# Warm-up products behind the first phase sums, and five in each wait of the output weights' transposes

## The chip, the cores and the metric

The kernel runs on one core of a Trainium2 chip, as one program. The metric is the device time of one execution in microseconds, the median of several runs. The engines are TensorE (PE in the rows; PEld is its weight load), VectorE (DVE), ScalarE (ACT), GpSimd (POOL) and SyncE (SP), which issues the loads and stores.

## The reference

Four batches of 768 tokens with eight heads of 48 go through a recurrence with a complex decay, then through a dense gated layer whose output is linear in two products, and then through a layer with eight experts, of which each token takes one.

```
mag = np.sqrt(a_re * a_re + a_im * a_im)
scale = np.minimum(mag, 0.999) / (mag + 1e-06)
ar, ai = a_re * scale, a_im * scale
S_re, S_im = ar * S_re - ai * S_im + k_t v_t, ar * S_im + ai * S_re     # for each token t
y[t] = q_t @ S_re
x = (x @ w_a) * (x @ w_b) @ w_out                                       # dense layer
do = x @ w_skip > 0                                                     # experts
e = argmax(x @ w_gate); gate = softmax(x @ w_gate)[e]
out = x + do * gate * (relu(x @ w1[e]) @ w2[e])
```

The inputs of the dense layer, w_a, w_b and w_out, arrive as 64-bit floats; the kernel reads them as pairs of 32-bit integers and puts the 32-bit value together itself.

## The kernel before

**The recurrence** is done in chunks of 128 tokens: 24 units of one chunk of one batch (number i), taken as 12 pairs (number g). For a unit, `att_exp` makes the logarithms of the decay and sums them over the tokens on TensorE (bank `l2_i`); `att_trig` makes the phases with Arctan and sums them (bank `tp_i`, line 251), then takes sine and cosine (`ts`) and rotates q and k (`qr`, `kr`, on VectorE). `att_pe` transposes the rotated q and k in two halves (banks `pq` and `pk`, lines 320 and 325), lets ScalarE copy them (`tq`, `tk`, lines 322 and 327), multiplies them to scores (`pc`, line 330), which VectorE masks (`sc`, line 332), and multiplies by v (`y`, line 352; the state's products `ds`, line 303). Three other names: `t1`, `t2`, `t` are its work tiles, `re`, `im` and `imp` its loads.

**The weights of the dense layer** come in 18 chunks, in the order of the words d.. of the string START: six of w_a, six of w_b and six of w_out (a0, b1, b0, o0, a1, o1 and so on). `decode` takes ScalarE (line 381) and three steps of VectorE (lines 382, 386, 387) for one chunk, 128 x 768 elements (tiles `deca`, `decb`, `deco`). `split` then rounds it on ScalarE (line 392, tiles `wa`, `wb`, `wo`) and takes the rest on GpSimd (line 393). Only three tiles serve all decodes in turn, so that the fourth one (deco0) uses the tile of the first (deca0). A decode releases the load of the chunk three places later: `load_after` lets GpSimd copy one element of the decoded tile into the raw tile, and the load waits for that. A chunk of w_out has a tail: TensorE transposes each of its two halves (bank `wt`, three transposes, line 451), ScalarE copies them (`wtt`, line 453), TensorE multiplies the copy by the gate's weights (line 455) and VectorE copies the result (`w2s`, line 456).

**The dense layer** of a pair g is done in 12 steps, m g.0 to m g.11 in START: products of the exchanged tokens `xt` with w_a and w_b (bank `ab`, lines 509 to 511), their product (`asb`, `gh`, `gl`), and the products with w_out (bank `op`). The tokens of a pair are exchanged between partitions by six transfers (`xt<-xt`, line 371).

**What sets the order.** START sets the order in which the code is written; a scheduler then orders each engine's instructions by its own estimates, with the table HOLD, which ties some instructions behind others. Each engine runs its list in that order, and so do the queues of loads on SP and POOL. The groups 0 and 1 and all decodes are in START; the groups from 2 on follow in a loop, in which TensorE has the dense layer of group g and the recurrence of group g + 1 to do.

**Products that nobody reads.** There are two kinds already. With WARM = 2 two products stand behind unit 0's `ts` (line 477, bank `warm`), and `warm(name, ins, n)` puts n bf16 products of 128 x 256 behind an instruction, into a bank "op" (lines 664 to 669); it is used near 730 us, between the dense layer and the experts.

Of the kernel before, what the change touches and what calls it, by code (L numbers as in the profile page):

```python
# [49 lines left out]
FILLP = ()  # L50
WARMS = (10, 6, 24)
WARMX = (13, 8)
ENGINES = {getattr(mybir.EngineType, x) for x in ("PE", "Activation", "DVE", "Pool")}
GF = 5
SGN = ()
# [4 lines left out]
def kern(tc, q, k, v, a_re, a_im, w_a, w_b, w_out, w_skip, w_gate, w1, w2, out):  # L60
# [3 lines left out]
    with st:  # L64
# [8 lines left out]
        def bank(tag, name, bufs):  # L73
            return ps.tile([P, 512], F32, tag=tag, name=name, bufs=bufs)

        env = SimpleNamespace(at=("at", "at2"), n=0)

        def at(name):
            env.n += 1
# [157 lines left out]
        def att_trig(i):  # L237
            c, b = units[i]
            d = U[i]
            im = d["im"]  # L240
            t3 = ew.tile([P, W], F32, tag="t3", name=f"t3_{i}")
            t4 = ew.tile([P, W], F32, tag="t4", name=f"t4_{i}")
            tact(out=t4, in_=im, func=AF.Arctan)
            if c > 0:

                cr = ew.tile([1, W], F32, tag="cr", name=f"cr{i}", bufs=1)
                sync.dma_start(cr, carry[b])
                dve.scalar_tensor_tensor(out=t4[:1], in0=cr, scalar=-2.0 * math.pi, in1=t4[:1], op0=ALU.mult, op1=ALU.add)
            tp = at(f"tp_{i}")
            if i < SPL:  # L250
                pe.matmul(tp[:, :W], trit, t4, start=True, stop=True)
            else:
                hi, lo = parts(i, "t", ("t2", "t1"))
                act.activation(out=hi, in_=t4, func=AF.Copy, scale=INV2PI)
                dve.scalar_tensor_tensor(out=lo, in0=t4, scalar=INV2PI, in1=hi, op0=ALU.mult, op1=ALU.subtract)
                cumsum(tp, hi, lo)

            if i in OFF.get("magic", ()):
                act.activation(out=t3, in_=tp[:, :W], func=AF.Identity, bias=b_magic)
            else:  # L260
                dve.tensor_scalar(out=t3, in0=tp[:, :W], scalar1=MAGIC, scalar2=None, op0=ALU.add)
            dve.scalar_tensor_tensor(out=t3, in0=t3, scalar=MAGIC, in1=tp[:, :W], op0=ALU.subtract, op1=ALU.subtract)
            if c + 1 < NCH:
                carry[b] = dpool.tile([1, W], F32, name=f"carry{i}")
                sync.dma_start(carry[b], t3[127:128])
            if i < 6:
                tact(out=t4, in_=t3, func=AF.Abs)
            else:
                dve.tensor_scalar(out=t4.bitcast(I32), in0=t3.bitcast(I32), scalar1=0x7FFFFFFF, scalar2=None, op0=ALU.bitwise_and)
            tact(out=t4, in_=t4, func=AF.Sin, scale=-TWO_PI_IN, bias=b_hpi)  # L270
            ts = ew.tile([P, W], F32, tag="t1", name=f"ts{i}")
            d["ts"] = ts
            marks["ts", i] = tact(out=ts, in_=t3, func=AF.Sin, scale=-TWO_PI_IN)
            for nm in ("q", "k"):
                tag = "krl" if nm == "k" and i >= 6 and i % 2 else nm + "r"
                r = ew.tile([P, 2 * W + 32], F32, tag=tag, name=f"{nm}r{i}", bufs=1)
                if nm == "k":
                    pool.memset(r[:, 2 * W :], 0.0)
                    d["kf"] = r
                r = r[:, : 2 * W].rearrange("t (h x d) -> t h x d", x=2, d=D)  # L280
                src = d[nm].rearrange("t (h d) -> t h d", d=D)
                off(nm + "c", i).tensor_tensor(out=r[:, :, 0], in0=src, in1=t4.rearrange("t (h d) -> t h d", d=D), op=ALU.mult)
                e = off(nm + "s", i)
                ins = e.tensor_tensor(out=r[:, :, 1], in0=src, in1=ts.rearrange("t (h d) -> t h d", d=D), op=ALU.mult)
                if e is dve:
                    mark((nm + "r", i), ins)
                d[nm + "r"] = r

        xts = {}

        def att_pe(i):
# [2 lines left out]
            qr, kr, vt, ee = d["qr"], d["kr"], d["v"], d["ee"]  # L294
            sc, qT = [], []
            stt = state[b]
            def delta(prev=None):

                ds = at(f"ds{i}")
                for h in range(H):  # L300
                    for x in range(2):
                        l = d["kf"][:, 96 * h + 64 * x : 96 * h + 64 * x + 64]
                        ins = pe.matmul(ds[64 * x : 64 * x + 64, h * D : (h + 1) * D], l, vt[:, h * D : (h + 1) * D], start=True, stop=True).ins
                        if prev is not None:
                            after(ins, prev)
                        prev = ins
                return ds, prev
# [9 lines left out]
            for hh in range(2):  # L317
                pq = at(f"pq{i}_{hh}")
                for j in range(4):
                    pe.transpose(pq[:96, j * P : (j + 1) * P], qr[:, 4 * hh + j].rearrange("t x d -> t (x d)"), ident)  # L320
                tq = ew.tile([96, 512], F32, tag="tq", name=f"tq{i}_{hh}", bufs=2)
                mark(("tq", i, hh), act.activation(out=tq, in_=pq[:96], func=AF.Copy))
                pk = at(f"pk{i}_{hh}")
                for j in range(4):
                    pe.transpose(pk[:96, j * P : (j + 1) * P], kr[:, 4 * hh + j].rearrange("t x d -> t (x d)"), ident)
                tk = ew.tile([96, 512], F32, tag="tk", name=f"tk{i}_{hh}", bufs=2)
                mark(("tk", i, hh), act.activation(out=tk, in_=pk[:96], func=AF.Copy))  # L327
                pc = at(f"pc{i}_{hh}")
                for j in range(4):
                    last = pe.matmul(pc[:, j * P : (j + 1) * P], tk[:, j * P : (j + 1) * P], tq[:, j * P : (j + 1) * P], start=True, stop=True).ins  # L330
                s_ = ew.tile([P, 4, P], F32, tag="sc", name=f"sc{i}_{hh}", bufs=2)
                msk = mark(("sc", i, hh), dve.tensor_tensor(out=s_, in0=pc.rearrange("s (j t) -> s j t", t=P), in1=tri[:, None, :].to_broadcast([P, 4, P]), op=ALU.mult))
                sc.append(s_)
                qT.append(tq)
# [37 lines left out]
            if c + 1 < NCH:  # L372
                new_state(ds)
            del U[i]


        def decode(dst, raw, by_pool, k):
# [57 lines left out]
        def decode_w(k, dec, wtp, ahead=None):  # L435
# [12 lines left out]
            for x in range(2):  # L448
                pt = bank("at2", f"wt{f}_{x}", 2)
                for c in range(NCC):  # L450
                    pe.transpose(pt[:, c * P : (c + 1) * P], d[:, x, c * P : (c + 1) * P], ident)
                wt = wtp.tile([P, DM], F32, tag="cr", name=f"wtt{f}_{x}", bufs=1)
                act.activation(out=wt, in_=pt[:, :DM], func=AF.Copy)
                for c in range(NCC):
                    pe.matmul(pt[:, DM : DM + 10], wt[:, c * P : (c + 1) * P], wg[:, c], start=c == 0, stop=c == NCC - 1)
                dve.tensor_copy(w2[:, x], pt[:, DM : DM + 10])
            split(t[:, 0, :, DM:], t[:, 1, :, DM:], w2)

        def att_exps(p):
            table("natural_log_exp_and_others")  # L460
# [8 lines left out]
        def att_trigs(p):  # L469
            table("trig_and_small")  # L470
            for i in (2 * p, 2 * p + 1):
                att_trig(i)
            if p == 0 and WARM:

                wm = bank("op", "warm", 2)
                for x in range(WARM):
                    pe.matmul(wm[:, :DM], ident, U[0]["ts"], start=True, stop=True)
            for i in (2 * p, 2 * p + 1):
                att_pe(i)


        M = {}
# [18 lines left out]
        def moe1_step(g, f):  # L501
            xt = M[g][0]
            fs = slice((f % 2) * P, (f % 2 + 1) * P)
            ab = bank("ab", f"ab{g}_{f}", 2)
            for x, nm in enumerate("ab"):
                o = ab[:, x * 256 : (x + 1) * 256]
                for c in range(NCC):
                    wh, wl = (env.w[nm, f // 2][:, y, c, fs] for y in range(2))
                    pe.matmul(o, wl, xt[:, c, 0], start=c == 0, stop=False)  # L509
                    pe.matmul(o, wh, xt[:, c, 1], start=False, stop=False)  # L510
                    pe.matmul(o, wh, xt[:, c, 0], start=False, stop=c == NCC - 1)  # L511
            if len(pend) == 2:
                moe1_out(*pend.pop(0))
            asb = env.mp.tile([P, 256], F32, tag="asb", name=f"asb{g}_{f}")
# [146 lines left out]
            if last:  # L661
                warm("t", ins.ins, WARMS[2])

        def warm(name, ins, n):

            if n:
                wm = bank("op", f"warm{name}", 2)
                for x in range(n):
                    after(pe.matmul(wm[:, :CAP], ones, iota, start=True, stop=True).ins, ins)

        giu = cpool.tile([P, 2, NE], U32, name="giu")
        siu = cpool.tile([P, 2, NE], U32, name="siu")
# [241 lines left out]
        moe1_flush()  # L914
        att_next(2)
        env.at = ("at", "at2")
        for g in range(2, NG):
            if g + 1 < NG:
                att_exps(g + 1)
# [186 lines left out]
```

## Time and profile before

| | us |
|---|---|
| median of 3 runs | 889.76 (889.67 to 892.65) |
| profiled execution, its own time | 889.2 |
| profiled execution, span from the first to the last instruction | 887.2 |
| TensorE busy in the span | 830.7 (94%) |
| VectorE busy | 554.3 (62%) |
| ScalarE busy | 466.7 (53%) |
| GpSimd busy | 266.6 (30%) |

The own time holds some 2 us around the span. A busy TensorE is not TensorE at its highest clock: the clock that was granted stands beside it, as a share of 2.4 GHz, so that 0.50 is 1.2 GHz. The first two groups and the decodes fill the stretch up to about 150 us, the rest of the recurrence and of the dense layer that up to about 725, and the experts the rest.

### The profile page before, as it was taken

What the parts mean: (1) busy time and instruction counts of PE and PEld (TensorE: products, weight loads), DVE (VectorE), ACT (ScalarE), POOL (GpSimd) and SP (SyncE); (2) the same over time, 40 slices, a digit from 0 to 9 for tenths busy, and PEclk for the clock granted to TensorE, in tenths of its full rate; (3) what the DMA queues carried; (4) which work ended last, traced back from release to release, by engine and by line L of the source; (5) the groups of instructions that cost most, each with busy time, mean ns of one, the idle gap of its engine ahead of it and who ended that gap; (6) DMA issues with size and microseconds to landing.
All of it is one profiled execution on the core that took longest, in us unless ns stands there. A gap on an engine that the chain in (4) does not pass through costs nothing.

```text
span 887.2 us, 18318 instructions
## 1 busy us (share of the span) xinstructions
PE 830.7 (94%) x7051; PEld 802.6 (90%) x7051; DVE 554.3 (62%) x1293; ACT 466.7 (53%) x977; POOL 266.6 (30%) x313
## 2 busy tenths in 40 slices
PE   2678889999999999999999999999999999999995
PEld 0567778999999999999999999999999889999995
DVE  3789976648567395764947658394753444755551
ACT  5577555646556373564726646374443325455540
POOL 5275543104131020312103130031302214675751
PEclk9687899999999999999999999999999999999998
DMA  9789672223122131221413222120102319767600
GB/s 166 143 159 191 164 108 55 72 45 84 36 72 58 26 92 33 71 59 25 102 26 77 45 72 57 27 73 10 55 1 73 116 40 322 239 218 228 190 16 30
DMA packets 162800, 81.53 MB, mean 92 GB/s; under 512 B 132788, under 2 KB 148730, under 8 KB 162704
## 3 DMA queue, kind: packets, MB, share of 16 engines
q1 hardware_dynamic: 160656, 74.88, 36.0%
q0 software_dynamic: 2048, 5.40, 1.7%
q8 instruction: 57, 0.93, 0.4%
q14 instruction: 39, 0.32, 0.1%
HBM read 66.10 MB, written 12.61 MB: 89 GB/s over the span
## 4 chain that ended last, share of the span: by engine, by line
PE 81%; DMA 7%; DVE 3%; ACT 3%; SPq 2%; issue 2%; POOL 1%; POOLq 0%; DVEq 0%; ACTq 0%
PE ab L509 11%; PE ab L511 10%; PE ab L510 10%; PE op L493 5%; PE op L495 5%; PE op L494 5%; PE y L352 5%; PE pc L330 5%; PE eh L786 3%; PE eh L787 3%; PE eh L789 2%; PE eo L803 2%; PE eo L805 2%; PE eo L804 2%; DMA rawb<-in_moe_w_b_dram 2%; PE pq L320 2%
## 5 line engine op out<-in xcount | busy, mean ns | idle before, releaser
L509 PE MATMUL ab<-xt,wa 128*128 128x256 f32 x432 | 125.6, 291 | 4.4 <-DVE asb L516 2.4
L511 PE MATMUL ab<-xt,wb 128*128 128x256 f32 x432 | 124.2, 288 | 0.0
L510 PE MATMUL ab<-xt,wb 128*128 128x256 f32 x432 | 123.5, 286 | 0.0
L511 PE MATMUL ab<-xt,wa 128*128 128x256 f32 x432 | 123.3, 285 | 0.0
L509 PE MATMUL ab<-xt,wb 128*128 128x256 f32 x432 | 123.3, 285 | 0.0
L510 PE MATMUL ab<-xt,wa 128*128 128x256 f32 x432 | 122.9, 285 | 0.0
L516 DVE TENSOR_TENSOR asb<-ab,asb 128x256 f32<-128x256 f32 x144 | 60.1, 418 | 70.6 <-ACT asb L515 70.0
L493 PE MATMUL op<-wo,gl 128*128 128x394 f32 x288 | 99.7, 347 | 2.4 <-DVE tbl L660 2.1
L495 PE MATMUL op<-wo,gh 128*128 128x394 f32 x288 | 99.3, 345 | 0.0
L494 PE MATMUL op<-wo,gh 128*128 128x394 f32 x288 | 99.0, 344 | 0.0
L518 ACT ACTIVATE gh<-asb 128x256 fp32r<-128x256 f32 x144 | 59.8, 416 | 65.1 <-DVE asb L516 64.3
L515 ACT ACTIVATE asb<-ab 128x256 f32<-128x256 f32 x144 | 54.4, 378 | 72.3 <-PE ab L511 67.8
L509 PEld LDWEIGHTS ab<-xt,wa 128*128 128x128 f32 x432 | 82.8, 192 | 5.6 <-issue 3.0
L520 DVE TENSOR_TENSOR gl<-asb,gh 128x256 fp32r<-128x256 f32 x144 | 64.8, 451 | 32.5 <-ACT gh L518 32.3
L754 POOL TENSOR_TENSOR wq<-stg,wq 128x768 fp32r<-128x768 f32 x32 | 59.5, 1863 | 85.1 <-DMA xt<-xt 43.7
L510 PEld LDWEIGHTS ab<-xt,wb 128*128 128x128 f32 x432 | 82.4, 191 | 0.9 <-issue 0.9
L510 PEld LDWEIGHTS ab<-xt,wa 128*128 128x128 f32 x432 | 83.1, 192 | 0.0
L511 PEld LDWEIGHTS ab<-xt,wa 128*128 128x128 f32 x432 | 83.0, 192 | 0.0
L509 PEld LDWEIGHTS ab<-xt,wb 128*128 128x128 f32 x432 | 82.4, 191 | 0.3 <-issue 0.2
L511 PEld LDWEIGHTS ab<-xt,wb 128*128 128x128 f32 x432 | 82.0, 190 | 0.7 <-issue 0.7
L330 PE MATMUL pc<-tq,tk 96*128 96x128 f32 x384 | 55.6, 291 | 8.2 <-ACT tk L327 8.2
L792 ACT ACTIVATE hh<-eh 128x256 fp32r<-128x256 f32 x64 | 24.6, 384 | 67.8 <-PE eh L789 66.1
(229 smaller groups left out, 2139.2 us busy)
## 6 DMA issues: line engine op xcount, KB each, us to landing
stg<-in_moe_w_dram SPq DMA_DIRECT2D x28, 768.0 KB
re<-in_a_re_dram SPq DMA_DIRECT2D x24, 192.0 KB
v<-in_v_dram SPq DMA_DIRECT2D x24, 192.0 KB
k<-in_k_dram SPq DMA_DIRECT2D x24, 192.0 KB
q<-in_q_dram SPq DMA_DIRECT2D x24, 192.0 KB
rawo<-in_moe_w_out_dram SPq DMA_DIRECT2D x6, 768.0 KB
xd<-xr SPq DMA_DIRECT2D x24, 192.0 KB
out_dram<-xr SPq DMA_DIRECT2D x24, 192.0 KB
```

What stands on the lines that cost most here:

```text
L330: last = pe.matmul(pc[:, j * P : (j + 1) * P], tk[:, j * P : (j + 1) * P], tq[:, j * P : (j + 1) * P], start=True, stop=True).ins
L493: pe.matmul(o, gl[:, ts], wh, start=f == 0, stop=False)
L494: pe.matmul(o, gh[:, ts], wl, start=False, stop=False)
L495: i = pe.matmul(o, gh[:, ts], wh, start=False, stop=f == NF - 1)
L509: pe.matmul(o, wl, xt[:, c, 0], start=c == 0, stop=False)
L510: pe.matmul(o, wh, xt[:, c, 1], start=False, stop=False)
L511: pe.matmul(o, wh, xt[:, c, 0], start=False, stop=c == NCC - 1)
L515: act.activation(out=asb, in_=ab[:, :256], func=AF.Copy)
L516: dve.tensor_tensor(out=asb, in0=ab[:, 256:], in1=asb, op=ALU.mult)
L518: act.activation(out=gh, in_=asb, func=AF.Copy)
L520: dve.tensor_tensor(out=gl, in0=asb, in1=gh, op=ALU.subtract)
L754: lo.tensor_tensor(out=o[:, 1], in0=t, in1=o[:, 0], op=ALU.subtract)
```

## The change

Three settings come in. `WARMA = (105, 0)` puts a row of 105 bf16 products of 128 x 256 behind the phase sums of the first pair; its second number, behind unit 0's last work, is zero. `WARMT = (5, 0)` puts five bf16 products of 112 columns behind each half's transposes of an output weight chunk, into columns 400 to 512 of the same bank, which nobody reads, while the first two groups are under way (`env.busy`): 12 halves, 60 products. `WARMB` is empty and does nothing.

```
+WARMA = (105, 0)
+WARMT = (5, 0)
+WARMB = {}
...
             if i < SPL:
-                pe.matmul(tp[:, :W], trit, t4, start=True, stop=True)
+                last = pe.matmul(tp[:, :W], trit, t4, start=True, stop=True).ins
...
                 for c in range(NCC):
-                    pe.transpose(pt[:, c * P : (c + 1) * P], d[:, x, c * P : (c + 1) * P], ident)
+                    ins = pe.transpose(pt[:, c * P : (c + 1) * P], d[:, x, c * P : (c + 1) * P], ident).ins
+                if env.busy:
+                    fill(pt, WARMT[0], ins)
                 wt = wtp.tile([P, DM], F32, tag="cr", name=f"wtt{f}_{x}", bufs=1)
...
+        def fill(b_, n, ins, col=400, w_=112):
+
+            for x in range(n):
+                after(pe.matmul(b_[:, col : col + w_], ones, iota[:, :w_], start=True, stop=True).ins, ins)
...
             for i in (2 * p, 2 * p + 1):
-                att_trig(i)
+                ins = env.last = att_trig(i)
+            if p == 0:
+                warm("c", ins, WARMA[0])
             if p == 0 and WARM:
...
         moe1_flush()
         att_next(2)
         env.at = ("at", "at2")
+        env.busy = False
```

The scheduler counts the new products in, and so it orders the instructions of all engines anew from about 20 us up to the second group; from there on the orders are the same again. Three places matter below. The lines of the changed kernel are some 3 to 26 higher than those of before for the same statement.

TensorE, from the first pair's phase sums to the first scores, before (`warm` are the two old filling products, `pc` the scores):

```order
L251 MATMUL tp_0_260<-t4_0_258,trit_76 128x384
L251 MATMUL tp_1_280<-t4_1_278,trit_76 128x384
L477 MATMUL warm_297<-ts0_268,ident_66 128x384 x2
L320 MATMUL pq0_0_300<-ident_66,qr0_270 96x128 x4
L325 MATMUL pk0_0_307<-ident_66,kr0_273 96x128 x4
L320 MATMUL pq0_1_321<-ident_66,qr0_270 96x128 x4
L330 MATMUL pc0_0_314<-tq0_0_305,tk0_0_312 128x128 x4
```

and with the change, with the 105 pairs of a weight load and a product between:

```order
L254 MATMUL tp_0_260<-t4_0_258,trit_76 128x384
L254 MATMUL tp_1_280<-t4_1_278,trit_76 128x384
L695 LDWEIGHTS ones_118
L695 MATMUL warmc_297<-iota_114,ones_118 128x256
...
L695 LDWEIGHTS ones_118
L695 MATMUL warmc_297<-iota_114,ones_118 128x256
L498 MATMUL warm_403<-ts0_268,ident_66 128x384 x2
L326 MATMUL pq0_0_406<-ident_66,qr0_270 96x128 x4
L332 MATMUL pk0_0_413<-ident_66,kr0_273 96x128 x4
L326 MATMUL pq0_1_427<-ident_66,qr0_270 96x128 x4
L337 MATMUL pc0_0_420<-tq0_0_411,tk0_0_418 128x128 x4
```

The row stands between the phase sums and the old filling products; what follows it keeps its order up to the first scores and beyond.

ScalarE, from the last square of pair 1 (`t2_3`) to the copies of unit 0's transposes, before (`deco0` is the first output weight chunk, `wo0` its rounding):

```order
L205 ACTIVATE t2_3_613<-im3_166 128x384
L204 ACTIVATE t1_2_588<-re2_158 128x384
L322 ACTIVATE tq0_0_305<-pq0_0_300 96x512
L327 ACTIVATE tk0_0_312<-pk0_0_307 96x512
L322 ACTIVATE tq0_1_326<-pq0_1_321 96x512
L381 ACTIVATE deco0_474<-rawo0_201 128x768
L327 ACTIVATE tk0_1_333<-pk0_1_328 96x512
L126 ACT_TABLE_LOAD
L153 ACTIVATE t1_2_588<-t1_2_588,b_tiny_80 128x384
L153 ACTIVATE t2_2_589<-t1_2_588,b_eps_78 128x384
L392 ACTIVATE wo0_485<-deco0_474 128x2x384
```

and with the change:

```order
L208 ACTIVATE t2_3_739<-im3_166 128x384
L389 ACTIVATE deco0_580<-rawo0_201 128x768
L400 ACTIVATE wo0_591<-deco0_580 128x2x384
L207 ACTIVATE t1_2_714<-re2_158 128x384
L329 ACTIVATE tq0_0_411<-pq0_0_406 96x512
L334 ACTIVATE tk0_0_418<-pk0_0_413 96x512
L329 ACTIVATE tq0_1_432<-pq0_1_427 96x512
L334 ACTIVATE tk0_1_439<-pk0_1_434 96x512
L129 ACT_TABLE_LOAD
L156 ACTIVATE t1_2_714<-t1_2_714,b_tiny_80 128x384
```

The decode of deco0 stood behind the third copy and its rounding wo0 behind the table load; both stand now ahead of the square `t1_2` and of all four copies. On VectorE the three steps of deco0 have moved with them, ahead of unit 1's rotation (`qr1`) and of the first mask `sc0_0`. Later in ScalarE's list the copy `tk1_1`, which stood behind the rounding `wb0`, stands ahead of it.

SP's queue of loads and exchanges near 110 to 140 us, before (each weight chunk is four transfers, of which the first two or the last one stand here; `re7` and `imp6` are loads of units 7 and 6, `xt1` is the exchange of group 1):

```order
L175 DMA k5_1132<-in_k_dram 128x8x48
L425 DMA rawb5_1220<-in_moe_w_b_dram 48x3x512
L426 DMA rawb5_1220<-in_moe_w_b_dram 16x3x512
...
L425 DMA rawa5_1174<-in_moe_w_a_dram 48x3x512
L426 DMA rawa5_1174<-in_moe_w_a_dram 16x3x512
...
L175 DMA re7_2139<-in_a_re_dram 128x8x48
L175 DMA imp6_2130<-in_a_im_dram 128x8x48 x2
L175 DMA v5_1134<-in_v_dram 128x8x48
L371 DMA xt1_849<-xt1_849 16x512 x6
```

and with the change:

```order
L178 DMA k5_1278<-in_k_dram 128x8x48
L178 DMA re7_2305<-in_a_re_dram 128x8x48
L433 DMA rawa5_1320<-in_moe_w_a_dram 48x3x512
L434 DMA rawa5_1320<-in_moe_w_a_dram 16x3x512
...
L433 DMA rawb5_1366<-in_moe_w_b_dram 48x3x512
L434 DMA rawb5_1366<-in_moe_w_b_dram 16x3x512
...
L178 DMA v5_1280<-in_v_dram 128x8x48
L178 DMA imp6_2296<-in_a_im_dram 128x8x48 x2
L378 DMA xt1_975<-xt1_975 16x512 x6
```

`re7` has moved from behind the last two weight chunks to ahead of them, and these two have changed places. On VectorE, near the same place, the work on `xt1` has moved ahead of the look at `imp6`, and the chunk o3 is decoded earlier, b4 ahead of o4 and a5 ahead of b5.

## Rows read from the trace of the kernel before

**Rows 1.** Mean granted clock of the core over the span.

```profile
core 0: 887.2 us, clock 0.969
```

**Rows 2.** Windows by stage: start:end, length, busy by engine (count), PEclk, DMA share.

```profile
42.40:69.00 26.60, 21.01 (x144) 17.35 (x145) 23.89 (x36) 19.08 (x36) 18.63 (x18) 0.77 0.86 172
69.00:118.00 49.00, 40.52 (x292) 38.12 (x292) 48.84 (x67) 31.88 (x60) 26.58 (x25) 0.83 0.89 171
118.00:150.00 32.00, 27.75 (x230) 25.49 (x229) 20.53 (x34) 16.81 (x36) 14.27 (x17) 0.95 0.39 67
150.00:725.00 575.00, 572.33 (x5215) 562.07 (x5214) 358.34 (x955) 301.18 (x667) 105.16 (x144) 1.00 0.23 55
```

**Rows 3.** The same view: stretches of one clock level, three early, one late.

```profile
23.90:30.70 6.80, 4.20 (x12) 2.79 (x13) 5.11 (x11) 4.00 (x7) 0.18 (x1) 0.50 1.23 174
30.70:34.10 3.40, 0.81 (x8) 0.56 (x6) 2.89 (x4) 3.00 (x7) 3.28 (x3) 0.99 1.05 302
34.10:44.40 10.30, 9.62 (x73) 8.15 (x74) 7.17 (x11) 5.83 (x9) 1.55 (x5) 0.50 0.33 63
129.00:134.00 5.00, 5.00 (x33) 4.45 (x33) 5.00 (x7) 1.50 (x3) 1.94 (x2) 0.66 0.02 5
```

**Rows 4.** Timeline of PE: start, us, what, count [idle before, releaser].

```profile
17.22 2.93 PE L251 MATMUL tp<-t,trit 128*128 128x384 f32 x4 [2.80 <-ACT t L153]
26.50 2.92 PE L477 MATMUL warm<-ts,ident 128*128 128x384 f32 x4 [6.36 <-ACT ts L153]
...
30.80 0.60 PE L320 MATMUL pq<-ident,qr 128*96 128x128 f32 x4
33.98 2.03 PE L330 MATMUL pc<-tq,tk 96*128 96x128 f32 x8 [2.58 <-ACT tk L327]
```

**Rows 5.** Timeline of PE: 256-column products at the low and the high level.

```profile
64.30 0.41 PE L510 MATMUL ab<-xt,wa 128*128 128x256 f32 x1
64.51 0.41 PE L511 MATMUL ab<-xt,wa 128*128 128x256 f32 x1
...
730.16 2.78 PE L669 MATMUL warmt<-iota,ones 128*128 128x256 bf16 x24
```

**Rows 6.** Timeline of ACT at the first copies.

```profile
32.46 0.51 ACT L204 ACTIVATE t<-re 128x384 f32<-128x384 f32 x1
32.88 0.57 ACT L322 ACTIVATE tq<-pq 96x512 f32<-96x512 f32 x1
33.35 0.58 ACT L327 ACTIVATE tk<-pk 96x512 f32<-96x512 f32 x1
...
34.30 0.91 ACT L381 ACTIVATE deco<-rawo 128x768 f32<-128x768 f32 x1
...
41.25 0.85 ACT L392 ACTIVATE wo<-deco 128x768 fp32r<-128x768 f32 x1 [1.18 <-DVE deco L387]
```

**Rows 7.** Timeline of POOL, the rounding of wa0.

```profile
31.67 1.81 POOL L393 TENSOR_TENSOR wa<-deca,wa 128x768 fp32r<-128x768 f32 x1
```

**Rows 8.** Timeline of DVE, deco0's first step and kr of unit 1.

```profile
36.66 0.55 DVE L382 TENSOR_SCALAR deco<-deco 128x768 int32<-128x768 int32 x1
...
42.43 0.56 DVE L282 TENSOR_TENSOR kr<-k,t 128x384 f32<-128x384 f32 x1 [0.75 <-PE ds L303]
```

**Rows 9.** Groups of DVE, 69 to 118 us: count | busy us, mean ns.

```profile
L387 DVE SCALAR_TENSOR_TENSOR deco<-rawo,deco 128x768 int32<-128x768 int32 x4 | 6.8, 1698 | 0.0
L387 DVE SCALAR_TENSOR_TENSOR decb<-rawb,decb 128x768 int32<-128x768 int32 x3 | 4.9, 1647 | 0.0
...
L387 DVE SCALAR_TENSOR_TENSOR deca<-rawa,deca 128x768 int32<-128x768 int32 x3 | 2.9, 957 | 0.0
```

**Rows 10.** Waits from 118 to 150 us: us in total, times, longest.

```profile
DVE re L203 <- DMA re<-in_a_re_dram: 3.3, 1, 3.3
...
DVE immax L208 <- DMA imp<-in_a_im_dram: 2.3, 1, 2.3
...
PE ab L509 <- DMA xt<-xt: 1.7, 1, 1.7
```

More of the change, by code (lines that the diff above doesn't have):

```diff
@@ L74, in bank @@
             return ps.tile([P, 512], F32, tag=tag, name=name, bufs=bufs)
-        env = SimpleNamespace(at=("at", "at2"), n=0)
+        env = SimpleNamespace(at=("at", "at2"), n=0, busy=True)
         def at(name):
@@ L250, in att_trig @@
             if i < SPL:
-                pe.matmul(tp[:, :W], trit, t4, start=True, stop=True)
+                last = pe.matmul(tp[:, :W], trit, t4, start=True, stop=True).ins
             else:
+                last = None
                 hi, lo = parts(i, "t", ("t2", "t1"))
@@ L287, in att_trig @@
                 d[nm + "r"] = r
+            return last
         xts = {}
@@ L296, in att_pe @@
             stt = state[b]
+            first = None
             def delta(prev=None):
@@ L374, in att_pe @@
             del U[i]
+            return first
         def decode(dst, raw, by_pool, k):
@@ L454, in decode_w @@
                 for c in range(NCC):
-                    pe.matmul(pt[:, DM : DM + 10], wt[:, c * P : (c + 1) * P], wg[:, c], start=c == 0, stop=c == NCC - 1)
+                    ins = pe.matmul(pt[:, DM : DM + 10], wt[:, c * P : (c + 1) * P], wg[:, c], start=c == 0, stop=c == NCC - 1).ins
+                if env.busy:
+                    fill(pt, WARMT[1], ins)
+                    if f == 0:
+                        env.last = ins
                 dve.tensor_copy(w2[:, x], pt[:, DM : DM + 10])
             split(t[:, 0, :, DM:], t[:, 1, :, DM:], w2)
+        def fill(b_, n, ins, col=400, w_=112):
+            for x in range(n):
+                after(pe.matmul(b_[:, col : col + w_], ones, iota[:, :w_], start=True, stop=True).ins, ins)
         def att_exps(p):
@@ L478, in att_trigs @@
             for i in (2 * p, 2 * p + 1):
-                att_pe(i)
+                ins = att_pe(i)
+                if i == 0:
+                    warm("d", ins, WARMA[1], tri_r, tri_r)
         M = {}
@@ L504, in moe1_step @@
             ab = bank("ab", f"ab{g}_{f}", 2)
+            if g == 0 and env.busy:
+                fill(ab, WARMB.get(f"ab{f}", 0), env.last, 0, 256)
             for x, nm in enumerate("ab"):
@@ L510, in moe1_step @@
                     pe.matmul(o, wh, xt[:, c, 1], start=False, stop=False)
-                    pe.matmul(o, wh, xt[:, c, 0], start=False, stop=c == NCC - 1)
+                    env.last = pe.matmul(o, wh, xt[:, c, 0], start=False, stop=c == NCC - 1).ins
             if len(pend) == 2:
@@ L662, in slots, with warm @@
                 warm("t", ins.ins, WARMS[2])
-        def warm(name, ins, n):
+        def warm(name, ins, n, l=None, r=None):
             if n:
@@ L668, in warm @@
                 for x in range(n):
-                    after(pe.matmul(wm[:, :CAP], ones, iota, start=True, stop=True).ins, ins)
+                    o = wm[:, :CAP] if l is None else wm[:, :P]
+                    after(pe.matmul(o, ones if l is None else l, iota if l is None else r, start=True, stop=True).ins, ins)
         giu = cpool.tile([P, 2, NE], U32, name="giu")
```

3 lines of the change are left out of this document (2 added, 1 removed).

## The prediction

> **What bounds the kernel now.** First the mean clock over the span, 0.969 [rows 1], then the busy time by stage [rows 2]. From 150 to 725 us TensorE works 572.33 of 575.00 us at a granted clock of 1.00: this stage is TensorE's own, and whatever is won or lost before 150 us is carried to the end one for one. Between 69 and 118 us VectorE works 48.84 of 49.00 us and TensorE 40.52 at a clock of 0.83: there VectorE sets the pace and TensorE's time is cheap. From 42.4 to 69 us VectorE still has 26.60 - 23.89 = 2.71 us idle, and from 118 to 150 us TensorE has 32.00 - 27.75 = 4.25 us idle. So the change can pay in two places, before 69 us and in the tail after 118 us.
>
> The clock rows [rows 3] show the two levels. From 23.9 to 30.7 us it is 0.50 (1.2 GHz); TensorE first idles there and works without a break from 26.50 [rows 4]. Then it is 0.99 (2.4 GHz), though TensorE worked only 0.81 of those 3.40 us, and from 34.1 it is 0.50 again, for 10.3 us in which TensorE worked 9.62. The timeline of TensorE [rows 4] says what it did before that: an idle stretch of 2.58 us ahead of the scores at 33.98, while ScalarE copied the transposes.
>
> **The long row: its price.** 105 bf16 products of 256 columns, each behind a weight load. At the high level the same form ran 24 times in 2.78 us, 0.116 us each; at the low level a product of 256 columns starts 64.51 - 64.30 = 0.21 us after the one ahead [rows 5]. Bounds: 105 x 0.116 = 12.2 us and 105 x 0.21 = 22.1 us. The phase sums begin at 17.22 and last 2.93 us [rows 4], so the row starts at about 20.1 and ends between 32.3 and 42.2. Where the level rises inside it is not in the rows; two cases bear on it. After 26.50, in unbroken work, it rose 4.2 us later, at 30.7; after 34.1, with 0.68 us of gaps, 10.3 us later [rows 3, 4]. Counted from 20.1 the first gives 4.2 us at the low level, 20 products, and 85 x 0.116 = 9.9 us: an end at 34.2. The second gives 49 products in 10.3 us and 56 x 0.116 = 6.5: 36.9. The row has no gaps, so I take the first, 34.2. Behind it stand the two old filling products, 2.92 us at the low level [rows 4] and so 1.46 at the high one, and twelve transposes at 0.60 for four [rows 4], 1.8: they are done at 37.5 (40.2 in the second case) instead of 30.80 + 0.60 = 31.4.
>
> **What that delays.** Less than it seems, since ScalarE took the first transposes up only at 32.88 [rows 6]. But ScalarE's queue has changed, and it runs in order: the decode of the first output weights (deco0) and their rounding (wo0) now stand ahead of that copy. deco0 reuses the slot of deca0, which GpSimd reads until 31.67 + 1.81 = 33.48 [rows 7], and its data had landed by 34.30 at the latest, when it ran without a wait [rows 6]. So it starts between 33.5 and 34.3 and takes 0.91. wo0 waits for VectorE's three decode steps, 0.55 [rows 8] and twice 0.957 [rows 9], 2.46 in all, and takes 0.85; behind it come the square t1_2 (0.42 from start to start) and the two copies tq0_0 and tk0_0 (0.47 each) [rows 6]. The first scores start at 33.5 + 0.91 + 2.46 + 0.85 + 0.42 + 0.94 = 39.1, or at 39.9, instead of 33.98: I take 39.5, **+5.5 us**. The row's end lies inside that: by itself it would put the copy of tq0_0 at about 36, and ScalarE gets there only at 38.5. Queued behind wo0 on ScalarE are all copies of the pair's first unit; behind deco0 on VectorE are the rotations of unit 1 (qr1), which TensorE asks for later.
>
> TensorE is then idle from 37.5 to 39.5, 2.0 us; before, an idle 2.58 us ended the high level [rows 4]. The gap is shorter now and the unbroken work ahead of it four times as long (17.2 to 37.5 against 26.5 to 31.4), so in my forecast the level holds; that it falls is rival 1. VectorE's next tie to TensorE is kr1, which waits for the state products (before at 42.43, after 0.75 idle [rows 8]). It would come 5.5 us late, but at the high level the 9.62 us of work from 34.1 to 44.4 [rows 3] halve and 4.8 come back; the other 0.7 goes into VectorE's 2.7 us of idle time up to 69 us [rows 2]: **0 us** is left when VectorE's full stretch starts. Bounds: if the level falls and the idle time takes 2.7 of 5.5, +2.8; if that idle time is of no use, +5.5. A gain is excluded, since VectorE's own work fills the rest. The copy tk1_1, which stood behind the rounding wb0, now stands ahead of it; that gain is TensorE's alone and VectorE hides it.
>
> The Trainium skill, TensorE: Matmul & The Clock Gate, "What's actually happening", says that the penalty of the ramp is under 1% of a typical span and warns against fitting anything to a count of cold products, since the count differs from run to run. By that the clock is worth at most 8.9 us here and a row of 105 is fitted to chance. The mean clock of 0.969 [rows 1] is 887.2 x 0.031 = 27.5 us, because the level falls again and again, so the row disagrees on the size; by that the ceiling of what warm products can bring is three times as high. My sum uses neither, since VectorE's full stretch stands between.
>
> **The fives.** Twelve transposed halves with five products of 112 columns each, 60 in all. No row has this form. Bounds: 0 where TensorE waits anyway, and 0.116 each, the price of 256 columns at the high level [rows 5], 7.0 us in all. Each five stands between transposes and the products that need ScalarE's copy of them, and lies in that wait; 40 of the 60 come before 118 us, under VectorE's full stretch. I take 0, the nearer row being the wait; if the last 20 were bare, 2.3.
>
> **The tail.** From 118 us VectorE stood 3.3 us on the load of re7, 2.3 us on imp6, and TensorE's products of the second group 1.7 us on xt1 [rows 10]. On the queue of loads re7 now goes out ahead of the last two weight chunks instead of behind them, and VectorE finishes xt1 before it looks at imp6. TensorE can win no more there than its idle 4.25 us [rows 2] and what the low level from 129 to 134 cost, 5.00 x (1 - 0.66) = 1.7 [rows 3]: 5.95 at most, and 0 at least, since the last chunk is now wb5, whose load is released by deco4's decode, and the stall may only move there. The three stalls add up to 7.3 us in one chain, more than TensorE's idle time, so I take that whole, and leave the level out, since some pause will stay: **-4.2 us**.
>
> **Sum.** The profiled execution's own time is 889.2 us, 2.0 over its span. 0 + 0 - 4.2: **885.0 us**. The median of before is 889.76, 0.56 higher; that is inside the forecast's own spread. Half a per cent is 4.45 us, about what a measurement of this kernel can tell from no change: 884.8 and 893.7 are the marks, counted from 889.2.
>
> **Rivals.**
> 1. The level falls in the idle stretch before the first scores, and the row's warmth is lost where it was made. For it: the row only has to end 0.6 us sooner for a gap of 2.6 us, and its bound of 32.3 makes it 4. Against it: the second case, a late end at 36.9, closes the gap. Then +2.8 is left: 889.2 + 2.8 - 4.2 = 887.8.
> 2. VectorE's full stretch changes its length. L387 took 957 ns on the mean for one kind of weights and 1698 and 1647 for the other two, the same shape [rows 9]; that lengthening is 4 x 0.74 + 3 x 0.69 = 5.0 us, and the new order deals it anew. Half of it gone, with the forecast: 882.5; half as much again: 887.5. Against it: the mix of engines there stays the same. The Trainium skill, GPSIMD Engine Reference, lists GpSimd's SBUF interface as shared with VectorE and in contention with instructions that have two inputs there; L387 is one, and its spread agrees, but these rows don't show what GpSimd did.
> 3. Slower: ScalarE's block on wo0 is the whole story. The stall of 5.5 at the first scores passes VectorE's idle time, because each later idle stretch is itself a wait that moves along, and the tail's stall moves to wb5. It decides from the point where less than 1.0 of the 2.7 is taken up and the tail gives nothing: 889.2 + 5.5 = 894.7, with the last 20 fillers bare 897.0.
> 4. It does nothing: the row fills idle time that nobody waits for, and what is lost early is won late: 889.
>
> **How the numbers follow.** Forecast 0.35, rival 1 0.15, rival 2 0.20, rival 3 0.20, rival 4 0.10. Faster than 884.8: somewhat more than half of the forecast (0.22), since the tail may also win back its 1.7 us of level, down to 883.3; a fifth of rival 1 (0.03); most of rival 2 (0.17): together 0.42. Slower than 893.7: rival 3, 0.20. Same: 0.38. The forecast alone has 882.5 to 887.5. The whole range reaches from the forecast with its 1.7 us of level and all of the 5.0 us of lengthening gone, 878.3, to a little past rival 3, 895.5, with a third of its bare fillers.
>
> **What would show it.** In the profile after: the row's first product near 20.1 and its last between 33 and 37; deco0 on ScalarE near 34 and wo0 near 37; the first scores near 39.5 and a clock near 1 behind them (0.50 in rival 1); VectorE full from about 69 to 118; no wait on re7 and none on xt1 after 118; TensorE without idle time from about 146. The prediction is wrong if the first scores start before 37 (then deco0 does not block), if VectorE's full stretch changes its length by over 3 us, or if the tail shows as much idle time on TensorE as before.

## The result, and the profile after

The change makes the kernel slower: 901.72 us median of 4 runs (899.62 to 904.67) against 889.98 of the kernel before, a ratio of 1.0127 (95% interval 1.0108 to 1.0147). The forecast was 885.0 us with a range of 878.3 to 895.5. (The ratios in this document come from all runs and are not quotients of the medians.) The profiled execution has a span of 900.2 us, 13.0 more than before, at a mean clock of 0.974 against 0.969 [rows 1]. Over all runs the clock is no higher: 0.970 to 0.976 in the four of the change, 0.969 to 0.978 in the 25 runs of the kernel before that stand beside the first experiments.

The windows by stage of the changed kernel (the same stretches as [rows 2]) show where the work is missing.

```profile
42.40:69.00 26.60, 18.99 (x159) 14.16 (x158) 17.33 (x28) 13.69 (x23) 7.07 (x11) 0.69 0.68 126
69.00:118.00 49.00, 42.16 (x318) 39.06 (x318) 41.37 (x60) 31.62 (x61) 28.04 (x24) 0.84 0.72 141
118.00:150.00 32.00, 23.59 (x223) 22.34 (x223) 26.43 (x39) 18.09 (x36) 15.86 (x17) 1.00 0.54 127
150.00:725.00 575.00, 573.08 (x5202) 562.15 (x5201) 361.09 (x960) 305.64 (x675) 111.71 (x151) 0.99 0.24 56
```

The long stage is as full as before (573.08 of 575 us); it ends later since it begins later (the row `warmt` behind it starts at 743.50 us, before at 730.16 [rows 5]). VectorE's full stretch is gone: 41.37 of 49 us where it was 48.84, and 17.33 of 26.6 us ahead of it where it was 23.89. It has hardly less to do in all (548.5 us in the span for 554.3); it waits, and the work slides into the stretch after 118 us (26.43 for 20.53).

The timeline of TensorE of the changed kernel, at the places of [rows 4], and the clock on both sides of the first scores:

```profile
17.39 2.93 PE L254 MATMUL tp<-t,trit 128*128 128x384 f32 x4 [2.80 <-ACT t L156]
20.12 13.30 PE L695 MATMUL warmc<-iota,ones 128*128 128x256 bf16 x105
33.26 1.46 PE L498 MATMUL warm<-ts,ident 128*128 128x384 f32 x4
...
35.42 0.60 PE L326 MATMUL pq<-ident,qr 128*96 128x128 f32 x4
41.73 2.08 PE L337 MATMUL pc<-tq,tk 96*128 96x128 f32 x8 [5.71 <-ACT tk L334]
```

```profile
36.02:40.70 4.68, 0.00 (x1) 0.00 (x0) 3.41 (x5) 2.01 (x4) 0.76 (x2) 0.99 0.03 4
40.70:50.90 10.20, 8.49 (x64) 7.36 (x66) 2.52 (x5) 5.09 (x9) 2.43 (x3) 0.50 0.61 96
```

The row costs about what was forecast: 13.30 us and an end at 33.42 (14.1 and 34.2). Its first 17 products start in 3.38 us, 0.2 us apart as at the low level, the other 88 in 9.92 us, 0.11 us apart:

```profile
20.12:23.50 3.38, 3.38 (x17) 2.43 (x16) 0.90 (x2) 0.00 (x0) 0.00 (x0) 1.00 1.20 161
23.50:33.42 9.92, 9.92 (x92) 8.88 (x90) 6.77 (x15) 5.04 (x9) 2.00 (x3) 1.00 1.16 190
```

The clock column says 1.00 in both. The trace's records of the level begin only at 23.5 us (in the kernel before at 20.4), and the column takes what lies ahead of them for full clock; there the spacing of the products tells the level.

But the first scores start at 41.73, not at 39.5, after an idle stretch of 5.71 us, and the level falls by 40.7, just ahead of them.

ScalarE's timeline of the changed kernel says why, twice:

```profile
35.90 0.89 ACT L389 ACTIVATE deco<-rawo 128x768 f32<-128x768 f32 x1 [1.67 <-DMA rawo<-in_moe_w_out_dram]
39.46 0.85 ACT L400 ACTIVATE wo<-deco 128x768 fp32r<-128x768 f32 x1 [2.67 <-DVE deco L395]
40.21 0.51 ACT L207 ACTIVATE t<-re 128x384 f32<-128x384 f32 x1
40.62 0.57 ACT L329 ACTIVATE tq<-pq 96x512 f32<-96x512 f32 x1
...
62.92 0.58 ACT L370 ACTIVATE xt<-y 128x512 fp32r<-128x512 f32 x1
68.01 0.89 ACT L389 ACTIVATE deca<-rawa 128x768 f32<-128x768 f32 x1 [4.52 <-DMA rawa<-in_moe_w_a_dram]
68.80 0.48 ACT L463 ACTIVATE wtt<-wt 128x384 f32<-128x384 f32 x1
69.17 0.84 ACT L400 ACTIVATE wo<-deco 128x768 fp32r<-128x768 f32 x1
69.90 1.63 ACT L156 ACTIVATE t<-l 128x384 f32<-128x384 f32 x4
```

deco0 waited for its load, and the copies of unit 0 stood behind it and wo0. At 63.5 ScalarE stood still once more, 4.52 us, on the data of a1; behind that decode stood the copy wtt0_0, wo1 and the last logarithm step of pair 1 (t<-l). In the kernel before, a1 was decoded after wtt0_0 and the logarithms, with only wo1 behind it. The chain that ended last runs in the changed kernel through the load of deco0 (at 30.40) and that of a1 (at 62.40), whose release waited for the load of o1 (at 56.55):

```profile
30.40 5.42 DMA rawo<-in_moe_w_out_dram
35.90 0.90 ACT deco L389
...
56.55 4.18 DMA rawo<-in_moe_w_out_dram
...
62.40 5.43 DMA rawa<-in_moe_w_a_dram
68.01 0.90 ACT deca L389
```

The kernel before's chain has the load of a1 too, 6.4 us earlier, but not that of deco0; near 33 us it runs through the copies:

```profile
32.97 0.48 ACT tq L322
...
56.01 6.48 DMA rawa<-in_moe_w_a_dram
```

### The profile page after: what moved, and what is told of

Its sections match the earlier page's. It is cut to its first block, busy times and chain, and to the rows that moved or that the text cites. A ratio compares the mean times of both kernels' runs of the same rounds, so it can differ in the third digit from the quotient of the medians.

```text
span 900.2 us, 18657 instructions
## 1 busy us (share of the span) xinstructions
PE 843.8 (94%) x7216; PEld 814.1 (90%) x7216; DVE 548.5 (61%) x1293; ACT 467.0 (52%) x977; POOL 265.4 (29%) x313
## 4 chain that ended last, share of the span: by engine, by line
PE 78%; DVE 7%; DMA 7%; ACT 3%; issue 2%; SPq 2%; POOL 1%; POOLq 0%; ACTq 0%; DVEq 0%
PE ab L534 10%; PE ab L536 10%; PE ab L535 10%; PE op L516 5%; PE op L518 5%; PE op L517 5%; PE y L359 4%; PE pc L337 4%; PE eh L812 3%; PE eh L813 2%; PE eh L815 2%; PE eo L829 2%; PE eo L830 2%; PE eo L831 2%; DMA rawb<-in_moe_w_b_dram 2%
## 5 line engine op out<-in xcount | busy, mean ns | idle before, releaser
L337 PE MATMUL pc<-tq,tk 96*128 96x128 f32 x384 | 53.0, 283 | 9.5 <-ACT tk L334 9.5
L339 DVE TENSOR_TENSOR sc<-pc,tri_r 128x512 f32<-128x512 f32 x48 | 33.0, 688 | 43.6 <-PE pc L337 43.3
```

## The experiments

The change does two things at once: it adds 165 products, and it makes the scheduler order all engines anew. To part them, a function behind the code of group 5 ties every instruction of an engine behind the one that is to stand ahead of it, as order alone, without a wait:

```
+            for e, order in ORD.items():
+                seq = []
...
+                    for i in own[e][int(a) : int(b or a) + 1]:
+                        seq += [i, *behind.get(i.name, ())]
+                for x, y in zip(seq, seq[1:]):
+                    after(y, x)
```

`own` holds an engine's instructions as the code writes them, `ORD` the places at which they stood in one kernel or the other, and `behind` the added products, which go where their own instruction is. With it the order of either kernel is had with or without products. Ratios are to runs of the kernel before on the same chip.

**Order against products.** Order of before with all products (old_order_all, with WARMA 105 and WARMT 5):

> All 165 products of the change, but every engine keeps the order that the kernel before has, up to the end of group 5 (each instruction is tied behind the one that stood ahead of it there). Theory A, the order: the new order of the engines' lists is what costs, not the products. Then this is within 888 to 892 us; the first scores start near 36.5 us (the row ends at 33.4, 1.46 of old fillers and two transposes behind it, then two copies), 2.5 us late, which VectorE's 2.7 us of idle time before 69 us takes up. Theory B, the products: the row holds TensorE late and the fives stand bare in the waits. Then 898 to 903 us.

Measured: 890.8 us, ratio 1.0007 (0.9985 to 1.0029). New order without any product (new_order_none, with WARMA 0 and WARMT 0):

> None of the 165 products, but every engine has the order that the scheduler made for the changed kernel, up to the end of group 5. Theory A, the order: 898 to 903 us, first scores still after 39 us, since ScalarE has the decode and rounding of deco0 ahead of the copies, and the exchange of xt0 goes out behind the load of rawo2, after 66 us. Theory B, the products: 888 to 892 us.

Measured: 901.64 us, ratio 1.0109 (1.0076 to 1.0142). That settles it: the order is the loss, and in the old order the products cost nothing that can be told from noise. TensorE's timeline of the run without products has the same late scores, with no row at all:

```profile
26.94 2.93 PE L508 MATMUL warm<-ts,ident 128*128 128x384 f32 x4 [6.71 <-ACT ts L164]
...
41.62 2.08 PE L345 MATMUL pc<-tq,tk 96*128 96x128 f32 x8 [9.30 <-ACT tk L342]
```

and that of the run with all products in the old order has them at 35.72, with 1.05 us of idle time ahead, close to the expected 36.5:

```profile
19.96 12.10 PE L705 MATMUL warmc<-iota,ones 128*128 128x256 bf16 x105
...
35.72 1.16 PE L345 MATMUL pc<-tq,tk 96*128 96x128 f32 x8 [1.05 <-ACT tk L342]
```

The row alone (old_order_row, WARMA 105 and WARMT 0) and the fives alone (old_order_fives, WARMA 0 and WARMT 5), both in the old order:

> The row of 105 alone, in the order of the kernel before. Theory A, the order: 888 to 892 us, as with all products. Theory B, the products: 892 us or more, by how much of the 5 us that the row moves the end of the transposes (31.4 to 36) comes through. If the level of the clock holds over the first scores, 886 to 888.

> The 60 products of 112 columns alone, in the order of the kernel before. Theory A, the order: 888.5 to 891 us, the fives lie in waits. Theory B, the products: 893 to 897 us, 60 times 0.07 to 0.12 us bare. If they keep the clock up between 54 and 118 us, the low stretches there are fewer than before.

Measured: 888.82 us, 0.9982 (0.9969 to 0.9995), and 891.29 us, 1.0008 (0.9991 to 1.0025). The row may be worth 0.2%, which is less than the half per cent that counts as a difference here; no worth of the fives shows.

**The head alone.** In the order of before, ScalarE's and VectorE's part of deco0 moved (old_head_new):

```
 ACTIVATE t2_3<-im3 128x384
+ACTIVATE deco0<-rawo0 128x768
+ACTIVATE wo0<-deco0 128x2x384
 ACTIVATE t1_2<-re2 128x384
...
-ACTIVATE deco0<-rawo0 128x768
 ACTIVATE tk0_1<-pk0_1 96x512
...
-ACTIVATE wo0<-deco0 128x2x384
```

> No new products, order of the kernel before, with one place changed: ScalarE's decode and rounding of deco0 and wo0 ahead of the square t1_2 and of all copies of unit 0, and VectorE's three steps of deco0 ahead of qr1, as in the changed kernel. First scores near 41.5 us. Theory H, the head: this block alone is the loss, 897 to 902 us. Theory M, the middle: the 7.5 us shrink by VectorE's idle time and the low level that the chip leaves earlier, 891 to 895 us, and the rest comes from the queues between 55 and 75 us. Theory T, the tail: 889 to 892 us.

Measured: 896.58 us, 1.0072 (1.0047 to 1.0097), between the ranges of theories H and M; first scores at 40.07 instead of 41.5. Neither all of the loss nor little of it. Its windows by stage:

```profile
42.40:69.00 26.60, 20.26 (x162) 15.85 (x161) 19.23 (x30) 18.09 (x31) 14.59 (x15) 0.76 0.66 122
69.00:118.00 49.00, 39.86 (x286) 37.63 (x285) 48.93 (x65) 32.27 (x59) 28.31 (x28) 0.81 0.83 170
118.00:150.00 32.00, 28.98 (x232) 26.21 (x230) 23.30 (x40) 16.82 (x37) 11.58 (x13) 0.95 0.59 91
```

VectorE's idle time from 42.4 to 69 us grew, from 2.71 to 7.37 us. A fixed window holds the shift too; in the window moved by the 6.1 us of the first scores it is 2.90 us, so nothing was taken up:

```profile
48.50:75.10 26.60, 20.94 (x144) 17.19 (x144) 23.70 (x36) 18.88 (x34) 18.70 (x18) 0.77 0.77 159
```

The 6.1 us at the first scores come out as 6.8 us at the end (4.2 to 8.6 by the interval).

**Repairs of the new order** were less clear. Its head put back (new_head_old: deco0, wo0, the release and load of rawa2 as in the kernel before):

> No new products, order of the changed kernel, with the head as before: deco0 behind the copy tq0_1, wo0 behind the first logarithms, on GpSimd and on the queue of loads the release and load of rawa2 where they were. First scores near 34 us. Theory H, the head: 888 to 892 us. Theory M, the middle: 895 to 899 us, with xt0 still behind the load of rawo2. Theory T, the tail: 898 to 902 us.

Measured: 897.7 us, 1.0076 (1.0049 to 1.0104): some 4 us of the 11 come back, as theory M has it and not H. The places between 55 and 75 us put back (new_mid_old), and both (new_both_old):

> No new products, order of the changed kernel, with the places between 55 and 75 us as before: the exchange xt0 ahead of the load rawo2, ScalarE's decode of a1 behind that of a2 and so no longer ahead of the copies and logarithms of pair 1, GpSimd's work on unit 2 and 3 ahead of the release of rawo2, rawb2 behind rawa3. First scores still near 41.5 us. Theory H, the head: 898 to 902 us. Theory M, the middle: 892 to 896 us. Theory T, the tail: 898 to 902 us.

> No new products, order of the changed kernel with both the head and the places between 55 and 75 us as before; what stays is the later order (o3 earlier, b4 ahead of o4, a5 ahead of b5, re7 ahead of the last two chunks). Theories H and M: 888 to 892 us. Theory T, the tail: 896 us or more. If the tail gives what was forecast, 884 to 886 us.

Measured: 907.6 us, 1.0202 (1.017 to 1.0234), and 902.76 us, 1.0147 (1.0109 to 1.0186). The first is slower than the order that it repairs (901.64), the second no faster than it and slower than with the head alone put back, against every theory. The rest of the new order decodes b2 before o2 and a3, and in both runs ScalarE waits 7.1 us for the data of b2, whose load was put back late; that this is the whole reason isn't shown. Single places moved in an order that was made as a whole tell little.

**By time.** So the two orders were joined at a time instead: what began before the cut in one kernel's profile stands first, in its order, and the rest follows in the other's.

> No new products. On every engine the instructions that began before 60 us in the run new_order_none stand first, in the new order; all others follow in the order of the kernel before. Theory H, the head alone costs: 900 to 902 us, all of the loss. Theory S, the loss has several places: 895 to 898 us, as in old_head_new, and the rest of the loss comes later.

> The same with the cut at 90 us, so with the new order of the queues of loads and of ScalarE between 55 and 90 us too. Theory H: 900 to 902 us as with the cut at 60. Theory S: 899 to 902 us, 3 to 5 us over the cut at 60, since the exchange xt0 behind the load rawo2 is in it.

> No new products. The instructions that began before 60 us in the profile of the kernel before stand first, in its order; all others follow in the new order. The head is whole, the new order of the middle and the tail is in it. Theory H: 888 to 892 us. Theory S: 893 to 897 us.

> The same with the cut at 118 us: only the tail has the new order, with re7 ahead of the last weight chunks where they had not gone out, b4, a5 and b5 as the changed kernel has them. By the term of the forecast for the tail, 4.2 us less: 884 to 888 us. If the tail's gain is not there or the stall only moves: 889 to 892 us. Theory S with a loss in the tail: over 893 us.

| order | us | ratio |
|---|---|---|
| new_to_60: new up to 60 us, then old | 894.61 | 1.0057 (1.0041 to 1.0074) |
| new_to_90: new up to 90 us, then old | 903.76 | 1.0158 (1.0136 to 1.018) |
| old_to_60: old up to 60 us, then new | 895.51 | 1.0064 (1.0047 to 1.0081) |
| old_to_118: old up to 118 us, then new | 890.51 | 1.0004 (0.999 to 1.0019) |

The two cuts at 60 us speak for theory S (the first a little under its range). The parts before and after 60 us add up, 0.57% + 0.64% = 1.21% against 1.27% of the change and 1.09% of the new order without products. The tail gives neither gain nor loss. With the cut at 90 us it is at or above the whole, over both theories; the old rest may fit the new middle worse than its own.

In new_to_60 the first scores start at 40.49, 6.5 us late, and 4.4 us of that are left at the end (3.6 to 6.6 by the interval). So a late start need not pass whole in every order.

**Which place between 55 and 90 us.** In the order of before, the load rawo2 ahead of the exchange xt0 (old_rawo2_first):

```
 DMA rawa1<-in_moe_w_a_dram 16x3x512
+DMA rawo2<-in_moe_w_out_dram 128x2x768
 DMA xt0<-xt0 16x512
...
-DMA rawo2<-in_moe_w_out_dram 128x2x768
```

> No new products, order of the kernel before with one place changed: on the queue of loads rawo2 stands ahead of the exchange xt0 as in the changed kernel, and GpSimd's release of rawo2 ahead of its work on unit 2 and 3. xt0 then goes out behind rawo2, near 62 to 65 us instead of 59.3. Theory Q, this queue place is the loss of the middle: first products ab near 67 to 69, 894 to 897 us. Theory A1, it is ScalarE's decode of a1: 889 to 892 us.

Measured: 891.11 us, 1.0015 (0.9997 to 1.0032): at most a part of it. Then chunk a1 (old_a1_early), here ScalarE's part (VectorE's steps, GpSimd's release and the load of rawb2 move with it):

```
 ACTIVATE deco1<-rawo1 128x768
+ACTIVATE xt0<-y1 128x4x128
+ACTIVATE deca1<-rawa1 128x768
 ACTIVATE wtt0_0<-wt0_0 128x384
-ACTIVATE xt0<-y1 128x4x128
+ACTIVATE wo1<-deco1 128x2x384
 ACTIVATE t1_2<-l2_2 128x384
...
-ACTIVATE deca1<-rawa1 128x768
-ACTIVATE wo1<-deco1 128x2x384
+ACTIVATE wa1<-deca1 128x768
...
-ACTIVATE wa1<-deca1 128x768
```

> No new products, order of the kernel before with one chunk moved: the decode of a1 (ScalarE, VectorE), its rounding, its release of rawb2 and that load stand where the changed kernel has them, on ScalarE ahead of the copy wtt0_0, of wo1 and of the logarithms of pair 1, and rawb2 goes out ahead of rawa3. ScalarE then waits for the data of a1, which land near 62.5 us. Theory A1: 894 us or more, rawa3 near 76 us or later instead of 68.3 and the later loads behind it. Theory Q: 889 to 892 us.

Measured: 902.26 us, 1.0141 (1.0112 to 1.017). Its two halves, the wait (old_a1_wait) and the load (old_b2_ahead):

> No new products, order of the kernel before; of old_a1_early only the engines' part: ScalarE's decode of a1 ahead of wtt0_0, wo1 and the logarithms of pair 1, VectorE's steps with it. GpSimd's release of rawb2 and its load stay where they were, behind rawa3. Theory W, ScalarE's wait for a1's data is the loss: 899 to 904 us, ScalarE idle near 7 us up to 62.5. Theory L, the place of the load rawb2 ahead of rawa3: 889 to 893 us.

> No new products, order of the kernel before; of old_a1_early only the load: rawb2 goes out ahead of rawa3, and GpSimd's release of it ahead of that of rawa3; all decodes stay. Theory W: 889 to 893 us. Theory L: 897 us or more, since rawa3 has to wait for the decode of a1, which ends near 69 us, and all later loads with it.

Measured: 898.98 us, 1.0112 (1.0082 to 1.0141), and 894.4 us, 1.0039 (1.0021 to 1.0058). Both cost, the wait most; the load's 3.7 us lie between the two theories, and its ten runs spread from 890.42 to 897.0. ScalarE's timeline of old_a1_wait:

```profile
57.05 0.60 ACT L378 ACTIVATE xt<-y 128x512 fp32r<-128x512 f32 x1 [0.44 <-PE y L367]
63.94 0.89 ACT L397 ACTIVATE deca<-rawa 128x768 f32<-128x768 f32 x1 [6.29 <-DMA xt<-xt]
64.73 0.48 ACT L471 ACTIVATE wtt<-wt 128x384 f32<-128x384 f32 x1
67.95 0.85 ACT L408 ACTIVATE wo<-deco 128x768 fp32r<-128x768 f32 x1 [2.74 <-DVE deco L403]
68.70 1.62 ACT L164 ACTIVATE t<-l 128x384 f32<-128x384 f32 x4
70.34 1.28 ACT L137 ACT_TABLE_LOAD   x1
```

The kernel before, at the same place:

```profile
56.42 1.64 ACT L153 ACTIVATE t<-l 128x384 f32<-128x384 f32 x4
58.08 1.28 ACT L126 ACT_TABLE_LOAD   x1
...
60.59 0.91 ACT L381 ACTIVATE deca<-rawa 128x768 f32<-128x768 f32 x1
63.02 0.91 ACT L381 ACTIVATE deca<-rawa 128x768 f32<-128x768 f32 x1 [1.53 <-DMA xt<-xt]
```

Before, ScalarE did pair 1's logarithms, the table load and another decode while the data of a1 came in, and waited 1.53 us. With a1 ahead it stands still for 6.29 us, and pair 1's last logarithm step starts 12.3 us later. (The profile names the exchange, which landed last of what it saw; the decode reads rawa.) The 2.74 us behind wo1 belong to this experiment alone: in the old order VectorE's last step of deco1 stands behind w2s0, which needs the copy behind a1. In the changed kernel, where that step stands ahead, wo1 has no such wait.

**Can warm products win anything?** A row of 55, which ends before the old fillers start, in the old order, without and with the fives (old_order_row55, old_order_row55_fives):

> A row of 55 instead of 105, no fives, order of the kernel before. It starts at 20 and ends near 27 us (4.2 us at the low level, 35 more at 0.116), just where the two old fillers started, which then take 1.46 instead of 2.92 us: the transposes are not held up. If warm products are worth anything here: 885 to 888 us. If VectorE and the loads set the pace whatever the clock: 888.5 to 891 us, like the row of 105.

> The same with the 60 products of 112 columns. If they keep the clock up without standing in the way: 885 to 888 us, at or below the row of 55 alone. If they are neutral as in old_order_fives: within 1 us of the row of 55.

Measured: 890.88 us, 1.0004 (0.999 to 1.0018), and 891.35 us, 1.0011 (0.9992 to 1.003). No. No version here beats the kernel before by half a per cent.

## Why the prediction was wrong

**The step that failed first** is the term of 0 us for the head. The sum brought +5.5 us at the first scores down to nothing in two parts: "at the high level the 9.62 us of work from 34.1 to 44.4 [rows 3] halve and 4.8 come back; the other 0.7 goes into VectorE's 2.7 us of idle time". Neither part came. The level was low behind the first scores, and in old_head_new the head's delay passed whole (6.1 us at the scores, 6.8 at the end): VectorE's idle time was a set of waits in the same chain, which moved along with it (2.90 us in the moved window for 2.71). That is the mechanism of rival 3, near its price (894.7 forecast; 896.58 with the head alone), with a chance of 0.20. But rival 3 calls the block the whole story, and it is about half. Where more of the order was new, less seems to come through: 4.4 us for scores 6.5 us late (new_to_60), and some 4 us back for scores 7.6 us earlier (new_head_old). What took up the rest there isn't shown.

**The block itself was right in kind and too small.** deco0 and wo0 did hold up the copies. deco0 started at 35.90 instead of 33.5 to 34.3, since its load landed at 35.82, later than the bound taken from the kernel before; the first scores came 7.75 us late for 5.5. In old_head_new it was 6.1.

**The clock.** The level was to hold over a gap of 2.0 us; the gap was 5.71, and the level fell by 40.7, as in rival 1. Whether a level that holds would have given 4.8 us back is open, since none held: with the row in the old order, where the gap was 1.05 us, it fell 2.3 us behind the first scores (last section). The under 1% that the prediction cites from the Trainium skill is said there of the ramp alone, so the 27.5 us of repeated falls do not contradict it.

**The middle was not looked at.** The working weighed only the head and the tail of the new order, and took tk1_1 ahead of wb0 as the one thing between. Half of the loss (0.64%, old_to_60) lies there. The working put it at nothing without a reason. The decode of a1 on ScalarE ahead of pair 1's work, waiting for data that were not there yet, makes 4.52 us of idle time in the changed kernel; in the old order the same move alone costs 8.2 us (old_a1_wait), and the load of rawb2 ahead of rawa3 another 3.7 (old_b2_ahead). How the two share the changed kernel's own 0.64% was not measured, since the rest of its order is built on them.

**The tail gave 0, not -4.2 us.** The waits named did go (on re7 0.4 us is left of 3.3, on imp6 and xt1 nothing): TensorE's idle time from 118 to 150 us fell from 4.25 to 2.19 us in old_to_118. But the row of windows is

```profile
118.00:150.00 32.00, 29.81 (x237) 28.47 (x237) 20.55 (x34) 15.61 (x37) 13.12 (x14) 0.89 0.40 73
```

with a clock of 0.89 where it was 0.95: 32 x 0.06 = 1.9 us of the low level in place of 2.1 us of idle time. ScalarE now waits 4.6 us for rawa there, which before was 3.5. Less idle time at a lower level takes no new order: old_order_all has the tail of before, with 3.2 us of wait on re7, and nearly the same row.

```profile
118.00:150.00 32.00, 29.86 (x249) 28.43 (x248) 20.29 (x33) 17.07 (x37) 14.49 (x16) 0.89 0.39 66
```

The term counted three stalls of one chain as if their sum were to be had, and took TensorE's idle time there as its price. With the tail of before that idle time is 2.14 us at a clock of 0.89, 4.25 at 0.95 and 5.86 at 1.00 (old_order_all, the kernel before, old_order_row55), at times that differ by less than half a per cent: in these three it goes with the level. In the changed kernel itself TensorE idles 8.41 us in this window.

**Rival 2's lengthening** did shrink, and bought nothing that shows: the last of VectorE's decode steps (line 387) takes 24.7 us over all 18 chunks in the kernel before, 22.3 in old_order_all, which is no faster, and 21.5 in the changed kernel.

**Right:** the price of the row (the forecast had 20 products at the low level, about 17 were), the fives at nothing, and that neither enters the sum by itself. The warning cited from the Trainium skill, TensorE: Matmul & The Clock Gate, "What's actually happening", against fitting anything to a count of cold products, is borne out: the same row took 13.30 us in the changed kernel, 12.10 in old_order_all and 11.74 in old_order_row, as more or fewer of its first products ran at the low level, and 105, 55 or no products make no difference of half a per cent in one and the same order.

## What to carry to other kernels

Where a scheduler counts products that nobody reads, adding them is a change of order on every engine; build both orders, and look in each for the in-order engine that now stands on a load ahead of work that others wait for, along the whole stretch that was ordered anew and not at its two ends. Tie the old order down to see what the products themselves are worth. Don't count the idle time of an engine inside a chain as a cushion: it can move with the chain. And read a stage's idle time together with its clock.

## What was not expected of the hardware

The clock can rise without the time falling. The windows from 24 to 150 us, which the records of the level cover whole, of the kernel before and of old_order_all, in this order:

```profile
24.00:150.00 126.00, 101.90 (x738) 91.15 (x739) 106.37 (x155) 80.14 (x150) 64.05 (x64) 0.81 0.74 140
```

```profile
24.00:150.00 126.00, 107.08 (x866) 97.43 (x865) 103.61 (x154) 79.70 (x149) 63.39 (x63) 0.86 0.74 139
```

The mean clock of this stretch is 0.86 for 0.81, 6.3 us of it, and the time is the same. Two single executions overstate it: over the whole span the mean is 0.979 in the ten runs of old_order_all and 0.9745 in the 25 of the kernel before beside them, some 4 us, at 890.8 and 890.58 us. Why this bought nothing isn't shown. The row also made the first scores 1.74 us late, and the low stretch behind them stayed. Nor is the clock without worth as such: among those 25 runs of one kernel the ones with the higher mean clock are the faster ones (correlation -0.55), though the record doesn't tell in which stage their level fell.

Nor does a long row keep the level up beyond it: in old_order_all TensorE worked without a break from 17.24 us to 34.66, then idled 1.73 us in two gaps (6.20 - 4.47), and the level fell at about 38.0, as the work began again behind the second gap:

```profile
31.90:38.10 6.20, 4.47 (x31) 3.37 (x29) 3.56 (x6) 4.52 (x10) 2.85 (x3) 0.99 0.72 176
38.10:44.90 6.80, 6.80 (x61) 5.78 (x62) 4.94 (x8) 4.04 (x6) 0.95 (x4) 0.51 0.35 76
```
